# Weight conversion on GpSimd in halves, a new order in the weighted sum, and a new plan of when attention, conversion and reloads are emitted

## The chip, the cores and the metric

The kernel runs on one core of a Trainium2 chip. The metric is the time of one execution in device microseconds. It was run three times; a profiled execution of its own gives the trace.

## The reference, cut to what matters

```python
# q, k, v: (2, 8, 576, 64) float32
scores = scale * np.matmul(q, k.transpose(0, 1, 3, 2))
kth = np.partition(scores, -32, axis=-1)[..., -32:-31]
scores = np.where(scores >= kth, scores, -1e9)
attn = softmax(scores)                       # exp(scores - max) / (sum + 1e-9)
x = np.matmul(attn, v)                       # -> (1152, 512): tokens x (heads * 64)
h = x @ w_in                                 # (512, 2048)
g = h * np.tanh(softplus(h))
x = g @ w_out                                # (2048, 512)
out = ((x @ w_a) * (x @ w_b)) @ w_out2       # 512 -> 1536 -> 512
```

The five weight matrices arrive as float64. The kernel gets their bits and makes float32 numbers of them on the chip.

## The kernel before, in words

**Attention.** The 1152 tokens make nine tiles of 128 rows: tiles 0 to 3 are batch 0, tiles 5 to 8 batch 1, and tile 4 holds the last 64 rows of both. A tile has four pairs of heads, so there are 36 pairs, numbered here 0 to 35; pairs 16 to 19 are tile 4. Per pair, TensorE makes the scores (`psc`, L175), ScalarE copies them to SBUF, and VectorE finds the 32 largest of each row by four rounds of `max` (L191) and three of `match_replace` (L194), then masks the exponentials (`e`, L212). TensorE transposes the masked rows in nine chunks of 128 columns (`pe`, L220), three to a PSUM bank; ScalarE copies each bank (`et`, L221), and TensorE multiplies with `v` into `px` (L227). Chunks 0 to 3 belong to the pair's first head, 5 to 8 to its second, chunk 4 to both. After a tile's last pair, `prs` (L241) spreads the row sums, and the tile's `x` is ready.

**The MLPs.** `PLAN` cuts the tiles into three blocks. Block 0 is the tiles [0, 1] and then [2], block 1 the tiles [3, 4, 5], block 2 the tiles [6, 7, 8]. For each block `gated` runs 16 chunks of the first MLP (once for [0, 1] and once for [2] in block 0; products `ph` L355, sums `acc` L362), and `bilinear` runs 12 chunks of the second (`ph`, sums `po`). The two gated groups of block 0 work in plain float32, the rest in split fp32r: each weight unit is made into a high and a low part by a copy (L327, or L325 on VectorE) and a subtraction on GpSimd (L328).

**The weights.** They come as 68 units of 128x512. `convert_` loads a unit's 64-bit words (L281, `w64`, three buffers), ScalarE scales the high words (L286) and the low words (L287) and takes the sign (L290), VectorE shifts (L288), GpSimd adds (L291) and multiplies with the sign (L292), and the unit is stored to DRAM (L299). `weight_` reloads it from there (`raw`, L318, `BUFS[2]` buffers), or, for the first units, takes it from the buffer `w` where it was made (`BUFS[1]` buffers). All DMAs are issued by SP's one queue, in order. A `w64` buffer is free for the load three units on only when L292 has read it.

**What sets the order.** `together` interleaves two streams by their counts: the quarter steps of attention (four to a pair, 144 in all) and the chunks of an MLP group. `STEPS` says how many attention steps are spread over each group. `chunk` emits conversions ahead of need, `CONV[2]` sixteenths of a unit more per chunk. The framework then orders each engine's instructions by priorities and a timeline of its own; the result is a fixed list for each engine, executed in order.

Of the kernel before, what the change touches and what calls it, by code (L numbers as in the profile page):

```python
# [14 lines left out]
ALU = mybir.AluOpType  # L15
# [4 lines left out]
U = 512  # L20
# [16 lines left out]
ABUF = (5, 3, 2, 1, 2, 3, 1, 2)  # L37
COPIES = (0, 0, 0, 1, 4, 2)

CONV = (26, 28, 15, 2)  # L40

STEPS = (28, 25, 20, 26, 13, 0, 5)

BUFS = (3, 11, 5, 6, 1)

WIDE = {2 * P: 2, P: 4}
NEG = -3.0e38


@with_exitstack  # L50
def topk_attention_mlps(ctx: ExitStack, tc: tile.TileContext, q, k, v, w, out):
# [6 lines left out]
    nc = tc.nc  # L58
# [5 lines left out]
    J = 4  # L64
# [22 lines left out]
    def bank(name, n=512):  # L87
        return ps.tile([P, n], F32, name=name, tag="bank", padded_shape=[P, 512])
# [4 lines left out]
    def load_v(b):  # L93
        vt[b] = const.tile([P, H, J, D], F32, name=f"v{b}")
        v4[b] = const.tile([P, NP, 2, D], F32, name=f"v4{b}")
        nc.gpsimd.memset(v4[b], 0.0)
        for h in range(H):
            nc.sync.dma_start(vt[b][:, h], v[b, h, 0:SM, :].rearrange("(p j) d -> p j d", j=J))
        for s in range(2):
            nc.sync.dma_start(  # L100
                v4[b][s * R:(s + 1) * R, :, s, :],
                v[b, :, SM:S, :].rearrange("(a s) p d -> s p a d", s=2)[s],
            )

    def prep_k(b, hp):
        ks = wp.tile([P, 2, J, D], F32, name="ks", bufs=BUFS[4])
        kr = wp.tile([R, 2, D], F32, name="kr", bufs=BUFS[4])
        for s in range(2):
            nc.sync.dma_start(ks[:, s], k[b, 2 * hp + s, 0:SM, :].rearrange("(p j) d -> p j d", j=J))
        nc.sync.dma_start(kr, k[b, 2 * hp:2 * hp + 2, SM:S, :].rearrange("h p d -> p h d"))  # L110
        km = wp.tile([P, 2, J, 2, D], F32R, name="km", bufs=BUFS[4])
        kn = wp.tile([R, 2, 2, D], F32R, name="kn", bufs=BUFS[4])
        for z, raw in ((km, ks), (kn, kr)):
# [66 lines left out]
    def largest(s2):  # L180
# [6 lines left out]
        for r in range(TOPK // 8):  # L187
# [4 lines left out]
            if r < TOPK // 8 - 1:  # L192
                for s in range(2):
                    nc.vector.match_replace(wk[:, s, :], m8[:, s, got], src[:, s, :], NEG)  # L194
            if r == 0:
# [9 lines left out]
    def weighted_sum_(t, hp, s2, wk, e2, kth):  # L205
        if hp == 0:
            if t in (0, J):
                load_v(t // J)
            XR[t] = att.tile([P, NP, P], F32, name="xr", bufs=2), att.tile([P, H], F32, name="sm")
        xr, sm = XR[t]  # L210
        for s in range(2):
            nc.vector.scalar_tensor_tensor(e2[:, s, :], s2[:, s, :], kth[:, s:s + 1], e2[:, s, :],  # L212
                                           op0=ALU.is_ge, op1=ALU.mult, accum_out=sm[:, 2 * hp + s:2 * hp + s + 1])
        et = att.tile([P, 2 * J + 1, P], F32, name="et", bufs=ABUF[3])
        ef = e2.rearrange("p s c -> p (s c)")
        for g in range(3):
            pe = bank("pe", 3 * P).rearrange("p (i t) -> p i t", t=P)
            for i in range(3):
                n = 3 * g + i
                nc.tensor.transpose(pe[:, i, :], ef[:, n * P:(n + 1) * P], ident)  # L220
            nc.scalar.copy(et[:, 3 * g:3 * g + 3, :], pe)  # L221
        px = bank("px", P)
        for b, o, n in ([(t // (J + 1), 0, P)] if t != J else [(b, b * R, R) for b in range(B)]):
            for j in range(J + 1):
                for s in range(2):
                    i = s * (J + 1) + j
                    nc.tensor.matmul(px[s * D:(s + 1) * D, o:o + n],  # L227
                                     vt[b][:, 2 * hp + s, j, :] if j < J else v4[b][:, hp, s, :],
                                     et[:, i if j < J else J, o:o + n],
                                     start=(j == 0), stop=(j == J), skip_group_check=True)  # L230
        nc.scalar.copy(xr[:, hp, :], px)
        if hp == NP - 1:
            with tc.high_priority(PRI[5]):
                rs = att.tile([P, H], F32, name="rs")
                x = xp.tile([P, NP, P], F32, name="x", bufs=4)
                nc.vector.tensor_scalar(rs, sm, 1e-9, None, op0=ALU.add)
                nc.vector.reciprocal(rs, rs)
                pr = bank("prs")
                for h in range(H):
                    o = h % 2 * D  # L240
                    nc.tensor.matmul(pr[o:o + D, h // 2 * P:(h // 2 + 1) * P], rs[:, h:h + 1].to_broadcast([P, D]),  # L241
                                     ident, start=True, stop=True, skip_group_check=True)
                nc.vector.tensor_mul(x, xr, pr.rearrange("p (c t) -> p c t", t=P))
                X[t] = x
# [27 lines left out]
    def convert(n):  # L272
        with tc.high_priority(PRI[4]):
            convert_(n)

    def convert_(n):

        while len(stored) < min(n, len(order)):
            key = order[len(stored)]
            w64 = wp.tile([P, U], mybir.dt.int64, name="w64", bufs=BUFS[0])  # L280
            nc.sync.dma_start(w64, w[:, len(stored), :])  # L281
            high, low, highf, count = (w64.bitcast(dt).rearrange("p (n t) -> p n t", t=2)[:, :, i]
                                       for dt, i in ((I32, 1), (U32, 0), (F32, 1), (I32, 0)))
            wf = wp.tile([P, U], F32, name="w", bufs=BUFS[1])
            wi = wf.bitcast(I32)
            nc.scalar.mul(wf, highf, 2.0 ** -112)  # L286
            nc.scalar.activation(count, low, AF.Copy, scale=2.0 ** -29)  # L287
            nc.vector.tensor_scalar(wi, wi, 3, 0x7FFFFFFF, op0=ALU.logical_shift_left, op1=ALU.bitwise_and)  # L288
            if len(stored) % 4 < SIGN[key[0]]:
                nc.scalar.activation(highf, highf, AF.Sign)  # L290
                nc.gpsimd.tensor_tensor(wi, wi, count, op=ALU.add)  # L291
                nc.gpsimd.tensor_mul(wf, wf, highf)  # L292
            else:
                nc.vector.scalar_tensor_tensor(wi, high, -0x80000000, wi, op0=ALU.bitwise_and, op1=ALU.bitwise_or)
                nc.gpsimd.tensor_tensor(wi, wi, count, op=ALU.add)
            if len(stored) < made[3] + BUFS[1] - 2:
                fresh[key] = wf
            stored[key] = dp.tile([P, U], F32, name=f"ws{len(stored)}")
            nc.sync.dma_start(stored[key], wf)  # L299

    def chunk():

        convert(CONV[1] + made[2] * CONV[2] // 16)
        made[2] += 1
# [68 lines left out]
    def gated(block, tiles, yt, at, split, second):  # L373
# [9 lines left out]
        acc = [ps_a.tile([P, DM], F32, name="acc", tag="acc") for _ in tiles]  # L383
        K = WIDE.get(T, 1)
        for f0 in range(0, F1, K):
# [80 lines left out]
    att_stream = attention()  # L466
    steps = iter(STEPS)
    together(attend(4 * NP * len(PLAN[0][0][0][0])), (converting(CONV[0]), CONV[0]))
    for i, (groups, s2, s3) in enumerate(PLAN):
# [41 lines left out]
```

## Time and profile before

| | |
|---|---|
| median of 3 runs (lowest, highest) | 801.2 us (799.43, 801.82) |
| the profiled execution | 802.57 us |
| its span | 800.8 us |
| TensorE (PE) busy | 689.9 us (86%) |
| VectorE (DVE) busy | 613.8 us (77%) |
| GpSimd (POOL) busy | 475.1 us (59%) |
| ScalarE (ACT) busy | 520.0 us (65%) |
| mean granted TensorE clock | 0.93 |

The busy shares are averages over a span whose first and last halves have different limits; the forty slices and the windows by stage are to be read before any average.

### The profile page before, as it was taken

The page shows a single profiled execution, that of the slowest core. Times are in us where ns is not written, and L with a number is a line of the kernel's source. Part 1 is how long each engine was busy: PE and PEld are TensorE (multiplying, and loading weights), DVE is VectorE, ACT ScalarE, POOL GpSimd, SP SyncE. Part 2 cuts the span into 40 slices and gives each one's busy share as a digit, 9 for nine tenths or more (in the row PEclk, how much of TensorE's full clock was granted, in tenths as well). Part 3 has the DMA queues.
Part 4 walks back from the last instruction along what each step waited for, and adds up shares of the span by engine and source line. Part 5 has one row for each costly group of instructions (what it writes and reads, how often), then busy time and mean ns, then how long its engine had stood idle before and what let it go on. Part 6 is the DMA issues. An engine that isn't in the chain of part 4 may idle for free.

```text
span 800.8 us, 12319 instructions
## 1 busy us (share of the span) xinstructions
PE 689.9 (86%) x3988; PEld 575.0 (72%) x3988; DVE 613.8 (77%) x1224; ACT 520.0 (65%) x1118; POOL 475.1 (59%) x390
## 2 busy tenths in 40 slices
PE   3565656698888799889999999997999999989997
PEld 2443535565656577679998888886889999969996
DVE  2999999989999999999788899999811265523332
ACT  5887778788899865655656688886533265553232
POOL 5676656677775740146656556773556767665661
PEclk9996666789999799989999999999999999989999
DMA  7987566689899754353324234331233454433431
GB/s 222 280 268 226 179 202 188 192 227 332 237 324 320 236 188 121 103 143 91 103 70 132 80 106 119 96 103 41 90 95 95 129 171 118 133 105 94 134 102 39
DMA packets 78816, 124.80 MB, mean 156 GB/s; under 512 B 27424, under 2 KB 31520, under 8 KB 78752
## 3 DMA queue, kind: packets, MB, share of 16 engines
q1 hardware_dynamic: 78752, 124.02, 51.5%
q8 instruction: 31, 0.51, 0.3%
q14 instruction: 33, 0.27, 0.1%
HBM read 103.81 MB, written 20.19 MB: 155 GB/s over the span
## 4 chain that ended last, share of the span: by engine, by line
PE 57%; DVE 21%; DMA 9%; ACT 6%; issue 3%; POOL 2%; SPq 1%; ACTq 0%; POOLq 0%; DVEq 0%
PE ph L355 29%; PE po L362 9%; PE acc L362 9%; DVE m L191 8%; DVE wk L194 6%; DMA w<-in_w_dram 6%; PE px L227 4%; DMA raw<-ws 3%; DVE e L212 3%; PE psc L175 2%; DVE w L288 2%; PE pe L220 2%; POOL w L292 1%; ACT w L286 1%; PE prs L241 1%
## 5 line engine op out<-in xcount | busy, mean ns | idle before, releaser
L328 POOL TENSOR_TENSOR whl<-raw,whl 128x512 fp32r<-128x512 f32 x161 | 214.7, 1342 | 162.3 <-ACT whl L327 123.6
L191 DVE MAX8 m<-wk 128x8 f32<-128x576 f32 x216 | 157.8, 748 | 0.9
L355 PE MATMUL ph<-yh,whl 128*128 128x384 f32 x576 | 157.4, 345 | 1.2 <-ACT yh L337 0.7
L291 POOL TENSOR_TENSOR w<-w,w 128x512 int32<-128x512 int32 x68 | 90.9, 1337 | 77.4 <-DVE w L288 49.7
L355 PEld LDWEIGHTS ph<-yh,whl 128*128 128x128 f32 x576 | 107.0, 193 | 4.9 <-ACT yh L337 1.0
L194 DVE MATCH_REPLACE8 wk<-m,wk 128x576 f32<-128x576 f32 x144 | 106.3, 740 | 0.0
L355 PE MATMUL ph<-yl,whl 128*128 128x384 f32 x288 | 98.7, 343 | 0.0
L292 POOL TENSOR_TENSOR w<-w,w 128x512 f32<-128x512 f32 x68 | 93.2, 1373 | 5.4 <-ACT w L290 1.2
L327 ACT CAST whl<-raw 128x512 fp32r<-128x512 f32 x110 | 67.9, 622 | 40.0 <-PE ph L355 17.2
L227 PE MATMUL px<-et,v 128*64 128x128 f32 (+1 forms) x800 | 78.9, 309 | 15.7 <-ACT et L221 15.6
L227 PEld LDWEIGHTS px<-et,v 128*64 128x64 f32 x800 | 57.0, 159 | 36.9 <-ACT et L221 21.9
L212 DVE SCALAR_TENSOR_TENSOR e<-s,m,e 128x576 f32<-128x576 f32 x72 | 77.6, 1085 | 0.9 <-ACT e L198 0.5
L370 POOL TENSOR_TENSOR gl<-m,gh 128x384 fp32r<-128x384 f32 x52 | 55.9, 1074 | 36.5 <-PE po L362 12.1
L220 PE MATMUL pe<-ident,e 128*128 128x128 f32 x324 | 56.3, 312 | 23.1 <-DVE e L212 15.6
L427 DVE TENSOR_TENSOR m<-ph,e 128x384 f32<-128x384 f32 x36 | 20.0, 556 | 70.7 <-PE ph L355 70.3
L369 ACT CAST gh<-m 128x384 fp32r<-128x384 f32 x68 | 34.8, 512 | 56.7 <-DVE m L427 36.2
L355 PE MATMUL ph<-xh,whl 128*128 128x384 f32 x256 | 71.3, 339 | 0.0
L175 PE MATMUL psc<-kks,qh 128*128 128x288 f32 x160 | 55.1, 364 | 17.7 <-ACT kks L126 8.9
L286 ACT ACTIVATE w<-w 128x512 f32<-128x512 f32 x68 | 46.1, 677 | 34.2 <-DMA w<-in_w_dram 22.5
L191 DVE MAX8 m<-s 128x8 f32<-128x576 f32 x72 | 53.5, 750 | 18.8 <-ACT s L177 18.6
L220 PEld LDWEIGHTS pe<-ident,e 128*128 128x128 f32 x324 | 44.7, 161 | 30.9 <-issue 8.5
L177 ACT COPY s<-psc 128x288 f32<-128x288 f32 x144 | 51.6, 402 | 16.0 <-PE psc L175 15.7
(87 smaller groups left out, 1484.7 us busy)
## 6 DMA issues: line engine op xcount, KB each, us to landing
raw<-ws SPq DMA_DIRECT2D x224, 256.0 KB, 2.7
w<-in_w_dram SPq DMA_DIRECT2D x68, 512.0 KB, 4.3
ws<-w SPq DMA_DIRECT2D x68, 256.0 KB, 4.5
qr<-in_q_dram SPq DMA_DIRECT2D x16, 256.0 KB, 4.0
ks<-in_k_dram SPq DMA_DIRECT2D x16, 128.0 KB, 3.8
v<-in_v_dram SPq DMA_DIRECT2D x16, 128.0 KB, 4.2
out_dram<-o SPq DMA_DIRECT2D x8, 256.0 KB, 2.6
qr<-in_q_dram SPq DMA_DIRECT2D x4, 128.0 KB, 5.5
```

The lines of the kernel that those rows point to most:

```text
L175: nc.tensor.matmul(psc, qq[:, s, :], kk[:, a * HS:(a + 1) * HS], start=(n == 0), stop=(n == len(parts) - 1))
L191: nc.vector.max(m8[:, s, got], src[:, s, :])
L194: nc.vector.match_replace(wk[:, s, :], m8[:, s, got], src[:, s, :], NEG)
L212: nc.vector.scalar_tensor_tensor(e2[:, s, :], s2[:, s, :], kth[:, s:s + 1], e2[:, s, :], op0=ALU.is_ge, op1=ALU.mult, accum_out=sm[:, 2 * ...
L220: nc.tensor.transpose(pe[:, i, :], ef[:, n * P:(n + 1) * P], ident)
L227: nc.tensor.matmul(px[s * D:(s + 1) * D, o:o + n], vt[b][:, 2 * hp + s, j, :] if j < J else v4[b][:, hp, s, :], et[:, i if j < J else J, o ...
L291: nc.gpsimd.tensor_tensor(wi, wi, count, op=ALU.add)
L292: nc.gpsimd.tensor_mul(wf, wf, highf)
L327: nc.scalar.copy(wh, raw)
L328: sub().tensor_sub(wl, raw, wh.bitcast(F32))
L355: nc.tensor.matmul(ph, a, x, start=(i == 0), stop=(i == len(mm) - 1))
L362: nc.tensor.matmul(acc[i], z[:, i * P:(i + 1) * P], a, start=(first and m == 0), stop=(last and m == len(mm) - 1))
```

## The change

GpSimd's add and multiply of a unit are each issued as two instructions on 256 columns (`PIECES`). The weighted sum takes the column chunks of `et` from the last to the first and the second head before the first, with the shared chunk last; the sum is the same, in another order of addition. `CONV[2]` goes from 15 to 20, `BUFS[1]` (buffers `w`) from 11 to 9, `BUFS[2]` (buffers `raw`) from 5 to 9, and `STEPS` spreads fewer attention steps over the two gated groups of block 0 and more over its bilinear group.

```diff
-CONV = (26, 28, 15, 2)
+CONV = (26, 28, 20, 2)
-STEPS = (28, 25, 20, 26, 13, 0, 5)
+STEPS = (24, 14, 32, 28, 14, 0, 5)
-BUFS = (3, 11, 5, 6, 1)
+BUFS = (3, 9, 9, 6, 1)
+PIECES = 2
...
         for b, o, n in ([(t // (J + 1), 0, P)] if t != J else [(b, b * R, R) for b in range(B)]):
-            for j in range(J + 1):
-                for s in range(2):
+            for nth, j in enumerate((*range(J - 1, -1, -1), J)):
+                for s in (1, 0):
...
-                                     start=(j == 0), stop=(j == J), skip_group_check=True)
+                                     start=(nth == 0), stop=(nth == J), skip_group_check=True)
...
+        pieces = [slice(i * U // PIECES, (i + 1) * U // PIECES) for i in range(PIECES)]
...
-                nc.gpsimd.tensor_tensor(wi, wi, count, op=ALU.add)
-                nc.gpsimd.tensor_mul(wf, wf, highf)
+                for z in pieces:
+                    nc.gpsimd.tensor_tensor(wi[:, z], wi[:, z], count[:, z], op=ALU.add)
+                for z in pieces:
+                    nc.gpsimd.tensor_mul(wf[:, z], wf[:, z], highf[:, z])
```

**TensorE, around `prs` of tile 4.** Line numbers in the change are a few higher (L227 is L230 there, L241 is L244, L355 is L362, L362 is L369). Before, the place reads:

```order
L227 MATMUL px<-et,v_331 64x64 x3
L241 MATMUL prs<-ident,rs 64x128 x8
L227 MATMUL px<-et,v_331 64x64 x5
L227 MATMUL px<-et,v_332 64x64 x2
L227 MATMUL px<-et,v_2611 64x64 x8
L227 MATMUL px<-et,v_2612 64x64 x2
L143 MATMUL pq<-ident,qr 128x128 x2
L362 MATMUL acc<-raw,m_3085 128x512 x4
```

In the change the same `prs` stands among the products of the bilinear group (`yl_1206` is the low part of its input):

```order
L362 MATMUL ph<-yl_1206,whl 128x384
L230 MATMUL px<-et,v_339 64x64
L244 MATMUL prs<-ident,rs 64x128 x8
L230 MATMUL px<-et,v_339 64x64 x7
L230 MATMUL px<-et,v_340 64x64 x2
L230 MATMUL px<-et,v_3024 64x64 x8
L230 MATMUL px<-et,v_3025 64x64 x2
L145 MATMUL pq<-ident,qr 128x128 x2
L369 MATMUL po<-whl,gl_3589 128x512 x3
```

Before, the sums of the gated group [2] (`acc`) still stand behind tile 4's last `px`; in the change both gated groups are done there, and products (`ph` from `yl`) and sums (`po`) of the bilinear group stand on the two sides of it.

**SP's queue, where the reloads of the first gated group begin** (the numbers at `w` and `ws` name buffers and DRAM tiles). Before:

```order
L299 DMA ws_1809<-w 128x512
L318 DMA raw<-ws_794 128x512
L281 DMA w_2026<-in_w_dram 128x512
L299 DMA ws_1828<-w 128x512
L281 DMA w_2045<-in_w_dram 128x512
L299 DMA ws_1937<-w 128x512
L318 DMA raw<-ws_809 128x512
L281 DMA w_2223<-in_w_dram 128x512
```

And in the change, where they begin two conversions earlier:

```order
L306 DMA ws_1639<-w 128x512
L325 DMA raw<-ws_856 128x512
L325 DMA raw<-ws_912 128x512
L285 DMA w_1764<-in_w_dram 128x512
L306 DMA ws_1660<-w 128x512
L285 DMA w_1832<-in_w_dram 128x512
L306 DMA ws_1741<-w 128x512
L325 DMA raw<-ws_957 128x512
L325 DMA raw<-ws_972 128x512
L285 DMA w_1853<-in_w_dram 128x512
```

Where one reload stood between two conversions, there are now often two. From the load of unit 38 to that of unit 68 the queue holds 30 reloads before and 52 in the change; in the whole program 224 and 229.

## Rows read from the trace of the kernel before

**Rows 1.** The page: busy time of each engine, and two lines of its 40 slices.

```profile
PE 689.9 (86%) x3988; PEld 575.0 (72%) x3988; DVE 613.8 (77%) x1224; ACT 520.0 (65%) x1118; POOL 475.1 (59%) x390
...
DVE  2999999989999999999788899999811265523332
...
PEclk9996666789999799989999999999999999989999
```

**Rows 2.** Windows by stage: busy us of each engine, clock, DMA share, GB/s.

```profile
core 0: us, PE busy (x) PEld busy (x) DVE busy (x) ACT busy (x) POOL busy (x), PEclk, DMA share, GB/s
140.00:300.00 160.00, 132.18 (x694) 94.77 (x695) 153.57 (x304) 134.64 (x282) 108.91 (x95) 0.89 0.83 257
350.00:601.00 251.00, 245.42 (x1542) 215.35 (x1540) 211.79 (x418) 166.35 (x370) 148.49 (x119) 0.99 0.33 93
601.00:800.80 199.80, 191.41 (x971) 174.47 (x970) 77.05 (x133) 81.62 (x160) 121.12 (x95) 0.98 0.38 112
```

**Rows 3.** Waits of PE and of DVE, 136 to 350 us (total, times, longest).

```profile
PE px L227 <- ACT et L221: 12.2, 6, 4.1
PE ph L355 <- DMA raw<-ws: 8.0, 7, 2.4
...
DVE w L288 <- POOL w L292: 2.7, 1, 2.7
```

**Rows 4.** Timeline of PE where the last `px` of pairs 16 and 20 run.

```profile
304.22 1.26 PE L227 MATMUL px<-et,v 128*64 128x64 f32 x34
...
347.48 1.68 PE L227 MATMUL px<-et,v 128*64 128x128 f32 x14
```

**Rows 5.** The window from pair 16's last `px` to pair 35's.

```profile
305.30:601.20 295.90, 283.15 (x1859) 244.32 (x1854) 255.06 (x514) 194.55 (x438) 157.34 (x126) 0.98 0.35 98
```

**Rows 6.** PE's price: chain, timeline, and two tiles (ns min/median/max).

```profile
648.76 2.10 PE ph L355 x12
650.86 2.08 PE acc L362 x9
...
301.25 1.06 PE L355 MATMUL ph<-xf,raw 128*128 128x128 f32 x8
170.73 5.31 PE L362 MATMUL acc<-w,m 128*128 128x512 f32 x12
...
L355 PE MATMUL ph<-xf,raw x216: 271/275/483, 167.5 to 325.4; 128*128 128x128 f32 x64, 128*128 128x256 f32 x44
L362 PE MATMUL acc<-raw,m x80: 590/592/894, 179.9 to 341.1; 128*128 128x512 f32 x80
```

**Rows 7.** DVE's first instruction of a gated set of 512 columns (busy, mean ns).

```profile
L397 DVE TENSOR_SCALAR e<-ph 128x512 f32<-128x512 f32 x12 | 8.1, 678 | 0.0
```

**Rows 8.** POOL's instructions by form (first two), then two of its timeline.

```profile
L291 POOL TENSOR_TENSOR w<-w,w 128x512 int32<-128x512 int32 x68 | 90.9, 1337 | 77.4 <-DVE w L288 49.7 <-ACT w L287 8.6 <-ACT w L290 4.7
L116 POOL TENSOR_TENSOR kn<-kr,kn 64x128 fp32r<-64x128 f32 x4 | 2.5, 630 | 0.0
...
8.79 1.28 POOL L291 TENSOR_TENSOR w<-w,w 128x512 int32<-128x512 int32 x1 [0.42 <-ACT kn L115]
10.03 0.45 POOL L116 TENSOR_TENSOR kn<-kr,kn 64x128 fp32r<-64x128 f32 x1
```

**Rows 9.** SP's queue: its longest wait, 140 to 300 us, and loads of units 38 and 68.

```profile
SPq L281 <- POOL w L292: 57.6, 29, 4.2
...
161.18 0.57 SPq L281 DMA_DIRECT2D w<-in_w_dram  x1
...
276.24 0.43 SPq L281 DMA_DIRECT2D w<-in_w_dram  x1
```

**Rows 10.** Windows of the conversion stretch, with DMA share and GB/s last.

```profile
161.00:276.20 115.20, 99.23 (x504) 68.27 (x504) 108.81 (x217) 102.04 (x212) 81.79 (x69) 0.92 0.89 278
...
200.00:250.00 50.00, 42.68 (x227) 29.31 (x228) 48.56 (x97) 44.60 (x93) 35.14 (x28) 0.97 0.92 279
220.00:230.00 10.00, 8.62 (x44) 5.14 (x40) 10.00 (x21) 9.31 (x18) 6.79 (x6) 1.00 1.01 372
```

More of the change, by code (lines that the diff above doesn't have):

```diff
@@ L290, in convert_ @@
                 nc.scalar.activation(highf, highf, AF.Sign)
-                nc.gpsimd.tensor_tensor(wi, wi, count, op=ALU.add)
-                nc.gpsimd.tensor_mul(wf, wf, highf)
+                for z in pieces:
+                    nc.gpsimd.tensor_tensor(wi[:, z], wi[:, z], count[:, z], op=ALU.add)
+                for z in pieces:
+                    nc.gpsimd.tensor_mul(wf[:, z], wf[:, z], highf[:, z])
             else:
                 nc.vector.scalar_tensor_tensor(wi, high, -0x80000000, wi, op0=ALU.bitwise_and, op1=ALU.bitwise_or)
-                nc.gpsimd.tensor_tensor(wi, wi, count, op=ALU.add)
+                for z in pieces:
+                    nc.gpsimd.tensor_tensor(wi[:, z], wi[:, z], count[:, z], op=ALU.add)
             if len(stored) < made[3] + BUFS[1] - 2:
```

## The prediction

> **What bounds the kernel now.** I read the page first [rows 1]. Its busy shares name no limit: TensorE has 86%, VectorE 77%. The slices do. VectorE stands at 9 almost without a break from slice 3 to about slice 18, a slice being 20 us, while TensorE's granted clock is often below 1, which is what an engine with gaps shows. From slice 18 on the clock is full and VectorE falls to 5 and below. So the kernel has two halves: first the top-k search on VectorE sets the pace, then TensorE's products do.
>
> The windows by stage make that a measure [rows 2]. From 140 to 300 us VectorE is busy 153.6 of 160 us and the clock is 0.89. From 350 to 601 us TensorE is busy 245.4 of 251 us at clock 0.99, and from 601 to the end nearly as much, with VectorE at 77 of 200. The waits agree [rows 3]: between 136 and 350 us TensorE waits 12.2 us for the copies of `et` and 8.0 us for reloads, and VectorE's longest wait is 2.7 us in all.
>
> A time is thus gained where TensorE's MLP work is moved from the second half into the gaps of the first, and lost where VectorE, before the handover, gets more to do or to wait for. I take the last `px` of pair 16 as the mark of the handover: it ends at 304.22 + 1.26 = 305.5 us; that of pair 20 ends at 349.2 [rows 4], and that of pair 35, the last, at 601.2, where the window of [rows 5] is cut. Behind pair 16 come 800.8 - 305.5 = 495.3 us.
>
> **The change part by part.**
>
> *Attention and MLP in another order (STEPS, CONV).* Both lists hold the same matmuls, but for a few that read `raw` in place of `w`; what differs is how many MLP products stand ahead of a given pair. I price them by TensorE's spacing [rows 6]: 2.10 / 12 = 0.174 us for a split product of 384 columns, 2.08 / 9 = 0.231 us for one of 512; a plain float32 product leaves two records, and from start to start I get (1.06 - 0.275) / 7 = 0.112 us at 128 columns and (5.31 - 0.59) / 11 = 0.429 us at 512 (the run without its last record, through the number of steps). A chunk of the gated group [2] has 8 of the first and 2 of the second, 1.75 us; a chunk of the bilinear group 24 x 0.174 + 9 x 0.231 = 6.26 us. Counted in the order, 73.6 us of MLP work stand ahead of pair 16's last `px` before and 84.9 us in the change: 11.3 us more, six and a half chunks of group [2], so both gated groups are done. At pair 20 it is 85.8 against 129.6 us, seven bilinear chunks more; at pair 35 the lists agree again within 0.2 us.
>
> So 11.3 us leave the stretch behind pair 16. Besides, between pairs 16 and 20 TensorE took 349.2 - 305.5 = 43.7 us for 12.2 us of MLP work and 25.5 us of attention, 6.0 us of it gaps. In the change 70 us of work stand there, so the gaps can be filled. Between 6.0 and nothing I take half, 3.0, since the copies that `px` waits for remain. Gain: 14.3 us if pair 16 comes no later.
>
> VectorE allows it: from 305.3 to 601.2 us it is busy 255.1 of 295.9 us [rows 5], so a stretch shorter by 14.3 still leaves it 26 us.
>
> *What makes pair 16 later.* The MLP's own VectorE work moves with it: ahead of pair 16's masks stand 2.5 more gated sets, each of two instructions of 0.68 us [rows 7] (the second taken as the first), 3.4 us, and one more search instruction, about 1 us. VectorE is the bound there, so all 4.4 us count.
>
> *GpSimd in halves.* No row has 256 columns, so I bound it [rows 8]. Undisturbed, 512 columns took 1.28 us and 128 columns 0.45, which is 2.16 ns a column and 0.73 us for 256: four make 2.92 where two made 2.56, +0.36 us a unit. By the means, 0.630 and 1.337, a half costs 0.87 and a unit 3.46 in place of 2.67, +0.79 us. GpSimd itself has room: 108.9 of 160 us [rows 2], and 40 units would add 14 to 32. But the conversion is a loop: SP's load of a unit waits for the multiply of the unit three before, 57.6 us in 140 to 300 us [rows 9]. Through three buffers a unit gets 0.12 to 0.26 us longer, over 30 units 3.6 to 7.9 us, if nothing in the loop has slack. Behind the waiting load stand the stores and the reloads, in SP's one queue; and VectorE's shift (L288), in order, holds up the search if its unit is late.
>
> *Reloads.* Nine buffers let SP run further ahead, two `w` buffers fewer make five reloads more, 224 to 229. What counts is where they stand: from the load of unit 38 to that of unit 68, 115 us before [rows 9], the queue has 22 more reloads of 0.262 MB, 5.8 MB. The stretch moved 278 GB/s x 115.2 us = 32.0 MB at share 0.89 [rows 10]; now it is 37.8 MB. At the rate of 200 to 250 us (279 GB/s at 0.92, so 303 at full share) this takes 125 us, 9.6 more; at the 372 GB/s of the best ten microseconds it takes 102, and nothing is added. The Trainium skill ("DMA: Bandwidth & Descriptors", Specifications) gives about 358 GB/s as the HBM limit of a core; by it the stretch would take 106 us, and the sum would have no term for the feed; the ten microseconds at 372 lie slightly above that figure, the mean of the stretch far below.
>
> Halves and reloads lengthen the same loop, so they cost the larger of the two and not both: 0 to 9.6 us. I take 2, near the low end, because the row nearest to it, VectorE's waits for the conversion at today's load, is 2.7 us in all.
>
> *The weighted sum backwards.* All ten products now wait for the last copy of `et`; before, the first three could go earlier, and the scheduler put the next `q` transposes behind them. Of TensorE's 12.2 us of waiting for `et` before the handover [rows 3] none sets the pace, and after it other products stand between. I count 0; the bounds are a gain of 3 us, the gaps that I left above, and a loss of as much.
>
> **The sum.** 800.8 - 11.3 - 3.0 + 4.4 + 2.0 = 792.9 us of span. The profiled execution took 802.57, 1.8 more than its span, and the median of the runs is 1.4 less than that; so 793 us as a median. About 0.3%, 2.4 us, is what a measurement of this kernel can tell from no change.
>
> **The rivals.**
>
> *The feed takes the gain back.* DMA is at 0.89 and VectorE at 94% of the conversion stretch [rows 10]; ask 18% more bytes of it and the reloads come late, TensorE's queue stands at a product, and scores and pair 16 with it. With the full 9.6 us instead of 2.0 the sum is 800.5 us of span, and if the gaps stay too, 803. For it speaks that the fifty microseconds at 0.92 moved only 279 GB/s; against it, that TensorE waited but 8.0 us for reloads and will have nine of them ahead. Chance 0.17.
>
> *VectorE stalls at the shifts: slower.* The change's order bunches the conversions: between the masks of pairs 10 and 13 VectorE has 18 shifts, where the densest three pairs before have 16. At (276.24 - 161.18) / 30 = 3.84 us a unit [rows 9] and 0.26 for the halves, 18 units take 73.8 us, against 61.4 for 16 today: 12.4 us, and VectorE, in order, can't search meanwhile. With the 4.4 us pair 16 then comes 16.8 us later, and the kernel takes 800.8 - 14.3 + 16.8 = 803.3 us, 806 if the gaps stay. It decides from a delay of pair 16 of 17 us on. For it speaks the wait of 57.6 us in SP's queue; against it, that a bunch can be followed by pairs with fewer units, in which the loop catches up, but VectorE can't get back what it lost. Chance 0.23.
>
> *More than I count.* From 140 to 300 us the clock is 0.89 of full [rows 2], which is 160 x 0.11 = 17.6 us of TensorE's time. If the denser products win back half of it, pair 16 comes 8.8 us earlier, and with all 6.0 us of gaps filled the sum is 781 us. For it speaks that more products stand in the same gaps; against it, that VectorE, which sets the pace there, gains nothing by the clock. Chance 0.15, within the faster ones.
>
> *The moves do nothing,* since the lists agree again at pair 35: it would need TensorE to have no gaps ahead of pair 20, against the gaps that [rows 4] show; I put it with the first rival.
>
> **How the numbers follow.** My case, 788 to 798, has 0.45 and the larger gain 0.15, so 0.60 for faster; the feed rival, centred on no change, is the 0.17 within 0.3%, and the stall is the 0.23 for slower. The range goes from 781 (the larger gain) to 805 (the stall, short of its worst end); the likeliest case alone has 788 to 798.
>
> **What would show it.** In the changed profile the last `px` of pair 16 should end at about 312 us, and from there to the end take about 481 us, with VectorE's window behind it busier than 86%. A half on GpSimd should take 0.73 to 0.87 us. The last load of a unit, at 276.2 us now [rows 9], should go out at 277 to 287. If pair 16 comes after 318 us, and VectorE's waits at L288 before 300 us exceed 10 us, the stall is right; if TensorE's waits for reloads grow beyond 15 us with a DMA share near 1, the feed is. If the tail behind pair 35, 199.6 us, has changed by more than 2 us, something moved that I have not seen.

## The result, and the profile after

| | before | changed |
|---|---|---|
| median of 4 runs (lowest, highest) | 800.32 us (799.31, 801.82) | 805.99 us (805.4, 807.11) |
| span of the profiled execution | 800.8 us | 803.7 us |

The ratio is 1.0078, with a 95% interval from 1.0055 to 1.01: slower, by more than the 0.3% that can be told from no change. The forecast said faster, 793 us. The two profiled executions lie 2.9 us apart, less than the medians; the accounts below are of these two.

The windows of the changed kernel, cut at the same stages as [rows 2] and at its own mark, the last `px` of pair 16 (columns as there):

```profile
core 0: us, PE busy (x) PEld busy (x) DVE busy (x) ACT busy (x) POOL busy (x), PEclk, DMA share, GB/s
140.00:300.00 160.00, 130.95 (x709) 95.37 (x706) 145.10 (x287) 136.92 (x282) 127.05 (x171) 0.92 0.88 289
604.10:803.70 199.60, 191.08 (x969) 174.18 (x968) 76.43 (x133) 82.40 (x160) 121.70 (x95) 0.98 0.36 106
314.00:604.10 290.10, 268.60 (x1807) 238.16 (x1802) 250.76 (x518) 185.64 (x426) 148.29 (x120) 0.96 0.31 86
314.00:410.00 96.00, 93.37 (x666) 86.39 (x661) 80.04 (x167) 54.95 (x127) 51.67 (x42) 0.98 0.35 92
410.00:570.00 160.00, 141.13 (x916) 122.58 (x915) 154.19 (x320) 115.83 (x268) 75.28 (x62) 0.94 0.30 86
```

The mark itself, on PE's timeline of the changed kernel (start, duration, both in us), answers to [rows 4]:

```profile
312.80 1.39 PE L230 MATMUL px<-et,v 128*64 128x64 f32 x40 [0.73 <-ACT et L223]
```

Pair 16 ends at 312.80 + 1.39 = 314.2 us, 8.7 later than before; 803.7 - 314.2 = 489.5 us follow in place of 495.3, 5.8 fewer. The forecast had 6.4 later and 14.3 fewer. The tail behind pair 35 is unchanged, 199.6 us.

The stretch from pair 16 to pair 35 tells where the gain went, set beside [rows 5]. TensorE's busy time fell from 283.15 to 268.60 us, 14.6, more than the 11.3 that I priced. Of that, 12.8 us are block 0's gated products (7.3 `acc`, 5.5 `ph`), which no longer stand behind the mark: the work did move ahead. Yet up to the mark TensorE's busy time rose by 4.1 us only (215.73 to 219.84, in the windows further down), for its `px` there cover 29.8 us in place of 41.5; the weighted sum, in the part on the prediction, comes back to this. But TensorE's idle time rose from 12.75 to 21.5 us, where I had let it fall by 3.0. And it is not idle where it used to be: before 410 us, in the stretch with the gaps that I wanted filled, 2.6 us are left; from 410 to 570 us it is idle for 18.9. In those two stretches VectorE does the opposite: it stands still for 16.0 of the first 96 us, and in the second it works 154.2 of 160. The kernel before, in the same 96 and 160 us behind its own pair 16, has TensorE idle for 7.9 and 4.9 us, and VectorE for 7.0 and 12.8:

```profile
305.30:401.30 96.00, 88.13 (x616) 75.21 (x612) 89.03 (x192) 56.84 (x133) 38.13 (x30) 0.95 0.39 108
401.30:561.30 160.00, 155.13 (x988) 134.92 (x987) 147.24 (x286) 120.45 (x268) 95.89 (x77) 1.00 0.33 94
```

The waits of PE in that stretch name the place (total us, times, longest), first of the changed kernel, 314 to 604 us:

```profile
PE psc L177 <- ACT qh L155: 6.3, 6, 2.4
PE psc L177 <- DVE ql L156: 6.1, 5, 3.1
PE px L230 <- ACT et L223: 4.1, 4, 1.7
PE ph L362 <- DVE yl L346: 1.8, 1, 1.8
```

and of the kernel before, 305 to 601 us:

```profile
PE px L227 <- ACT et L221: 4.8, 3, 2.1
...
PE psc L175 <- DVE x L243: 1.4, 1, 1.4
PE psc L175 <- ACT xr L231: 0.8, 1, 0.8
PE psc L175 <- ACT qh L153: 0.7, 1, 0.7
PE psc L175 <- DVE ql L154: 0.7, 2, 0.4
```

The scores (`psc`) wait for the two parts of the transposed queries (`qh`, `ql`): 1.4 us before, 12.4 now, 11.0 more. With what else the scores waited for before, 2.2 us in these lines and 0.3 for keys, the rise is 8.5, nearly all of the 8.75 us by which the idle time rose. One such wait on the changed kernel's two timelines, PE first, then DVE:

```profile
541.90 0.44 PE L145 MATMUL pq<-ident,qr 128*128 128x128 f32 x2
542.92 0.53 PE L177 MATMUL psc<-kks,qh 128*128 128x288 f32 x2 [0.58 <-ACT qh L155]
546.59 0.85 PE L177 MATMUL psc<-kks,ql 128*128 128x288 f32 x2 [3.14 <-DVE ql L156]
```

```profile
543.55 1.40 DVE L193 MAX8 m<-wk 128x8 f32<-128x576 f32 x2
544.88 0.66 DVE L246 TENSOR_TENSOR x<-xr,prs 128x512 f32<-128x512 f32 x1
545.47 0.75 DVE L193 MAX8 m<-wk 128x8 f32<-128x576 f32 x1
546.14 0.40 DVE L156 SCALAR_TENSOR_TENSOR ql<-pq,qh 128x256 fp32r<-128x256 f32 x1
```

The queries are transposed by 541.90 + 0.44 = 542.3 us. VectorE makes `ql` at 546.1, because the search, and once a tile's `x`, stand ahead of it in its queue; TensorE has no product in between and waits 3.14 us. The opposite happens earlier, on DVE's timeline of the same kernel:

```profile
407.93 0.76 DVE L193 MAX8 m<-s 128x8 f32<-128x576 f32 x1 [4.93 <-ACT s L179]
```

Here the search waits 4.93 us for scores, which stand in TensorE's queue among bilinear products. In all VectorE waits 11.5 us for scores between 300 and 420 us.

Ahead of pair 16, VectorE's windows up to the mark, before and changed:

```profile
0.00:305.50 305.50, 215.73 (x1168) 156.56 (x1169) 281.87 (x579) 243.81 (x520) 196.59 (x169) 0.85 0.78 240
```

```profile
0.00:314.00 314.00, 219.84 (x1221) 163.00 (x1221) 281.15 (x575) 251.94 (x533) 229.41 (x311) 0.88 0.79 255
```

VectorE has no more work there, 281.15 against 281.87 us; it stands still 9.2 us longer. Its waits from 137 us to pair 16, before and changed:

```profile
DVE w L288 <- POOL w L292: 2.7, 1, 2.7
DVE w L288 <- ACT w L286: 1.2, 1, 1.2
DVE w L288 <- POOL w L291: 1.1, 1, 1.1
DVE m L191 <- ACT s L177: 0.6, 2, 0.4
DVE w L288 <- issue: 0.5, 1, 0.5
```

```profile
DVE w L292 <- ACT w L290: 4.7, 6, 1.5
DVE m L409 <- ACT m L408: 3.2, 2, 1.8
DVE w L292 <- POOL w L298: 2.6, 2, 1.3
DVE w L292 <- issue: 1.0, 2, 0.7
```

The shifts of the conversion (L292, before L288) wait 8.3 us where they waited 5.5, and the gated sets 3.2 where they did not wait. From the start of the program the shifts wait 16.3 us, 13.7 before. GpSimd's halves, to be read beside [rows 8], took 800 ns:

```profile
L298 POOL TENSOR_TENSOR w<-w,w 128x256 f32<-128x256 f32 x136 | 106.1, 800 | 1.5 <-ACT xr L234 1.1 <-ACT w L294 0.4
```

### The profile page after: what moved, and what is told of

It is laid out like the page before. It is cut to its first block, busy times and chain, and to the rows that moved or that the text cites. A ratio compares the mean times of both kernels' runs of the same rounds, so it can differ in the third digit from the quotient of the medians.

```text
span 803.7 us, 12499 instructions
## 1 busy us (share of the span) xinstructions
PE 679.5 (85%) x3988; PEld 575.3 (72%) x3988; DVE 608.3 (76%) x1224; ACT 520.0 (65%) x1118; POOL 499.4 (62%) x526
## 5 line engine op out<-in xcount | busy, mean ns | idle before, releaser
L335 POOL TENSOR_TENSOR whl<-raw,whl 128x512 fp32r<-128x512 f32 x164 | 217.5, 1334 | 138.4 <-ACT whl L334 102.7
L362 PE MATMUL ph<-yh,whl 128*128 128x384 f32 x576 | 157.9, 344 | 0.7 <-ACT yh L344 0.7
L296 POOL TENSOR_TENSOR w<-w,w 128x256 int32<-128x256 int32 x136 | 106.0, 800 | 68.2 <-DVE w L292 37.8
L362 PEld LDWEIGHTS ph<-yh,whl 128*128 128x128 f32 x576 | 107.5, 193 | 3.9 <-ACT yh L344 1.5
L298 POOL TENSOR_TENSOR w<-w,w 128x256 f32<-128x256 f32 x136 | 106.1, 800 | 1.5 <-ACT xr L234 1.1
L362 PE MATMUL ph<-yl,whl 128*128 128x384 f32 x288 | 99.1, 344 | 1.8 <-DVE yl L346 1.8
L377 POOL TENSOR_TENSOR gl<-m,gh 128x384 fp32r<-128x384 f32 x52 | 57.5, 1106 | 41.5 <-ACT gh L376 13.9
L230 PE MATMUL px<-et,v 128*64 128x128 f32 (+1 forms) x800 | 59.4, 293 | 24.7 <-ACT et L223 24.7
L230 PEld LDWEIGHTS px<-et,v 128*64 128x64 f32 x800 | 47.9, 152 | 37.5 <-ACT et L223 30.3
L214 DVE SCALAR_TENSOR_TENSOR e<-s,m,e 128x576 f32<-128x576 f32 x72 | 72.8, 1014 | 1.4 <-ACT e L200 1.0
L362 PE MATMUL ph<-xh,whl 128*128 128x384 f32 x256 | 71.2, 340 | 1.2 <-DVE m L409 1.0
L177 PE MATMUL psc<-kks,ql 128*128 128x288 f32 x160 | 51.5, 362 | 17.7 <-DVE ql L156 17.6
L177 PEld LDWEIGHTS psc<-kks,qh 128*128 128x128 f32 x160 | 34.8, 228 | 41.9 <-ACT qh L155 30.7
```

The lines of the kernel that those rows point to most:

```text
L177: nc.tensor.matmul(psc, qq[:, s, :], kk[:, a * HS:(a + 1) * HS], start=(n == 0), stop=(n == len(parts) - 1))
L230: nc.tensor.matmul(px[s * D:(s + 1) * D, o:o + n], vt[b][:, 2 * hp + s, j, :] if j < J else v4[b][:, hp, s, :], et[:, i if j < J else J, o ...
L296: nc.gpsimd.tensor_tensor(wi[:, z], wi[:, z], count[:, z], op=ALU.add)
L298: nc.gpsimd.tensor_mul(wf[:, z], wf[:, z], highf[:, z])
L335: sub().tensor_sub(wl, raw, wh.bitcast(F32))
L362: nc.tensor.matmul(ph, a, x, start=(i == 0), stop=(i == len(mm) - 1))
```

## The experiments

In each, "before" is the kernel before on the same chip, in the same session; ratios are to it, with their 95% interval. Pair 11, 16 and 35 with a time mean the start of the last record of their `px` in the profiled execution, which is 0.2 to 0.3 us before its end; so counted, the kernel before has 305.3 and 601.2 for the last two, the changed one 314.0 and 604.1.

**One part undone in the source.** The first four put back `STEPS` (e1), whole units (e2) or `BUFS` (e3) in the changed kernel, or gave the kernel before the new `STEPS` (e4).

```diff
-STEPS = (24, 14, 32, 28, 14, 0, 5)
+STEPS = (28, 25, 20, 26, 13, 0, 5)
...
-PIECES = 2
+PIECES = 1
...
-BUFS = (3, 9, 9, 6, 1)
+BUFS = (3, 11, 5, 6, 1)
```

> The changed kernel with the old STEPS alone put back; in the order, 85 us of MLP work stand ahead of pair 20's last px, as before the change, where the changed kernel has 130. Theory of the order (the new STEPS put bilinear chunks of block 0 ahead of the attention of tiles 4 and 5, so VectorE starves at 360 to 420 us and TensorE later runs out of products at 420 to 450 and 520 to 560): the loss goes, 794 to 801 us, and TensorE is busy over 95% from pair 22 to pair 31. Theory of the feed (halves and reloads make pair 16 8.5 us later and this carries through to the end): 804 to 808 us, pair 16 at 312 us or later.

> The changed kernel with whole units on GpSimd (PIECES = 1). Theory of the order: 803 to 808 us, no measurable gain, with the same gaps at 420 to 450 and 520 to 560 us. Theory of the feed: pair 16 at 306 to 309 us and 798 to 802 us in all.

> The changed kernel with the old BUFS (5 reload buffers, 11 w buffers). Theory of the order: 803 to 808 us. Theory of the feed: fewer reloads ahead of the last conversions, pair 16 at 306 to 310 us, 798 to 802 us in all.

> The kernel before with the new STEPS alone. Theory of the order: it has the whole loss, 804 to 809 us, with TensorE short of products near pairs 23 to 25 and 30 to 31. Theory of the feed: 799 to 802 us, no change.

Measured: 816.19 us (1.0176 [1.0143, 1.0209]), 821.42 (1.025 [1.0225, 1.0275]), 830.49 (1.0362 [1.0336, 1.0387]) and 817.14 (1.0188 [1.0163, 1.0213]), before 801.12. All four miss what every theory expected: each mixture is slower than both kernels. One edit makes the framework order every engine anew, so these runs price a new order and not the part. From here on the order of every engine was written down and forced, and only the edits that are named were made in it.

**The changed order forced, and one edit undone in it.** e5 forces the changed kernel's own order; e6 has whole units in it, e8 the old order of the sum.

```diff
+    dep = mybir.DependencyInfo(mybir.DependencyClass.NoSync, mybir.DependencyReason.DATA)
...
+                if last is not None:
+                    tc.add_manual_dep(made[engine][at], last.name, dep, reason="pinned")
+                last = made[engine][at]
```

> The changed kernel with the order of every engine's instructions written down and forced, nothing else changed. It is the base for the runs that change one thing while no instruction moves. Both theories: 803 to 809 us, as the changed kernel (806.0), px of pair 16 at 312 to 316, of pair 35 at 602 to 606. Outside of that the forcing itself costs or gives something, and the pinned runs have to be read against this one alone.

> The changed kernel's order forced, but GpSimd converts each unit whole (one instruction of 512 columns in place of two of 256; the other engines' orders stay word for word). GpSimd is then 0.42 us a unit shorter for 68 units, 28 us in all. Theory A (the capped lead: behind pair 22 VectorE paces the attention and TensorE starves, the halves are a small price at the front): pair 16 at most 3 us earlier, the end 0 to 3 us earlier than the pinned base, 803 to 806. Rival B (the feed: the halves and the reloads delay the front and that is where the gain went): pair 16 6 to 10 us earlier and the end by as much, 796 to 800.

> The changed kernel's order forced; the weighted sum takes the transposed columns first to last again, as the kernel before did. Theory A: nothing that can be measured, within 2 us of the pinned base. Rival C (the backwards sum makes each px wait for the last eviction at its first matmul, where the forward order had eight matmuls to hide it): 3 to 8 us earlier than the pinned base, most of it between pairs 9 and 16 where px waits for et.

Measured, with before at 801.96: e5 805.07 (1.0043 [1.0025, 1.0062]), pair 16 at 315.1, pair 35 at 605.9: a fair base. e6 808.94 (1.0092 [1.0061, 1.0122]), pair 16 at 316.6; e8 805.78 (1.0053 [1.003, 1.0077]), pair 16 at 314.5. Both rivals fall: neither the halves nor the backwards sum make this order slower. Theory A missed e6 as well, by a little: whole units were to be as fast or faster. The same edit as in e2 costs 3.9 us where nothing moves, against some 14 there, by the ratios.

**Less search on VectorE.** e7 for pairs 23 to 31, e16 for every pair from 17 on, both in the changed order; e18 is the control in the order of before.

```diff
+            n = S // 2 if r and 17 <= i else S
...
-                nc.vector.max(m8[:, s, got], src[:, s, :])
+                nc.vector.max(m8[:, s, got], src[:, s, :n])
...
-                    nc.vector.match_replace(wk[:, s, :], m8[:, s, got], src[:, s, :], NEG)
+                    nc.vector.match_replace(wk[:, s, :n], m8[:, s, got], src[:, s, :n], NEG)
```

> The changed kernel's order forced; for pairs 23 to 31 the search's rounds after the first look at the first 288 of 576 columns only (so these pairs' sums differ from the reference), which takes some 3.7 us of VectorE's work from each of the 9 pairs and leaves all else alone. Nothing ahead of pair 23 changes. Theory A: TensorE stood idle for some 19 us between 418 and 564 us since VectorE could not bring products in time; it gets 10 to 19 us of it back: 787 to 796, and TensorE's busy share of 418 to 564 goes above 95%. Rival B: what is lost was lost ahead of pair 16, the end moves by less than 4 us, 802 or more.

> The changed kernel's forced order with the search's later rounds over the first 288 columns for every pair from 17 on (these pairs' sums differ from the reference), 70 us of VectorE's work in all. If VectorE's own work sets the pace behind pair 22: pair 16 to pair 35 falls from 290.8 to 270 to 277 us, the end to 786 to 793. If the order does (TensorE reaches instructions of the attention whose inputs come a fixed chain later, and has no product to put in between): TensorE still idles 10 us or more between 410 and 570 and the end is 796 to 800, hardly below the 800.3 of the run that cut pairs 23 to 31.

> The control for the short search: the kernel before with its own order forced and the search's later rounds over 288 columns for every pair from 17 on (these pairs' sums differ from the reference). In the changed order this gave 12.1 us. If the moves are what made VectorE the pace behind pair 16: here 0 to 6 us, 795 to 801, most of it ahead of pair 20 where VectorE was full. If VectorE paces either order alike: 10 to 14 us, 787 to 791.

Measured: e7 800.28 (0.9992 [0.9969, 1.0015]), 4.8 us below the base, between the two theories; the pairs around those nine kept their full search. e16 792.94 (0.991 [0.9885, 0.9936]), before 800.85. e18 797.45 (0.9959 [0.9934, 0.9983]), before 801.67, within what was expected if the moves made VectorE the pace. e16 lands between its two theories: its time is within the first one's bounds, at their upper end, and its stretch of 278.3 us just beyond them, but TensorE still idles 14.0 us between 410 and 570, as the second one said. The windows from pair 16 to pair 35 in e5, e16 and e18:

```profile
315.10:605.90 290.80, 267.64 (x1808) 237.47 (x1802) 250.84 (x518) 185.12 (x426) 149.05 (x120) 0.96 0.29 86
```

```profile
317.70:596.00 278.30, 263.28 (x1807) 234.63 (x1802) 204.94 (x516) 184.88 (x426) 148.10 (x120) 0.98 0.30 90
```

```profile
303.60:594.50 290.90, 279.75 (x1861) 242.69 (x1855) 203.35 (x507) 194.52 (x438) 157.52 (x126) 0.99 0.35 100
```

VectorE lost about the same work in both, 46 and 52 us of the stretch. In the changed order that makes the stretch 12.5 us shorter, in the old one 5.0 (from the 295.9 of [rows 5]). By the ratios the whole kernel gains 1.3% against its base in the one, 0.4% in the other; there the base is the kernel before as it was, since its order was not forced without an edit. So VectorE does set the pace behind pair 16 in the changed order, for the larger part, and only a little in the old one. The scores' wait for `qh` and `ql` in that stretch falls from 11.6 to 4.7 us, and TensorE's idle time from 23.2 to 15.0; the rest of it does not come from VectorE's amount of work.

**The products spread later.** e9 and e10 keep e5's instructions, but the MLP's stand later among the attention's, by this rule for the time t at which each ran:

```
e9:   t 335 -> 335, 410 -> 432, 460 -> 460, linear between
e10:  t 335 -> 335, 410 -> 432, 460 -> 460, 525 -> 545, 550 -> 550
```

> The changed kernel's forced order with one thing altered: the MLP's instructions that ran between 335 and 460 us (on all engines and in SP's queue) stand later among the attention's, up to 22 us at 410, so that 10 to 15 us less of the MLP's products lie ahead of pairs 20 to 22 and as much more ahead of pairs 23 to 25. Theory A, restated after the short search gave 4.8 us only: TensorE and VectorE take turns as the bound. From 340 to 410 TensorE is full and VectorE waits for scores, from 410 to 450 the products have run out and TensorE waits for the attention. Then TensorE's idle time between 410 and 460 falls from 7.8 us to 3 or less and the end comes 4 to 7 us earlier than the pinned base: 798 to 801. Rival B (the loss is that of the front alone, the order behind it costs nothing): within 2 us of the base, 803 to 807.

> As the run before, and the same for the second place: the MLP's instructions between 460 and 550 us stand up to 20 us later among the attention's, so that 7 to 11 us less of the products lie ahead of pairs 27 to 30 and the two pairs without any product (30 and 31) get some. Theory A: the idle 12 us between 510 and 570, and part of the low granted clock there, go as well: 786 to 794, below both kernels. If VectorE's own work is the bound from 440 to 570 (it is 18 to 20 of 20 us busy there), only the first place pays: 797 to 801. Rival B: 803 to 807.

Measured, before 802.61: 821.63 (1.0229 [1.0196, 1.0261]) and 825.9 (1.0291 [1.0261, 1.0321]); both theories miss. In e10 TensorE's idle time from 510 to 570 us did go, from 12.6 to 3.0 at full clock, but the gain was eaten elsewhere. The windows of e9 and e10 from pair 16 to pair 35 say where:

```profile
312.90:622.50 309.60, 287.40 (x1807) 242.74 (x1804) 254.25 (x518) 187.03 (x426) 151.18 (x120) 0.95 0.28 82
```

```profile
313.70:626.80 313.10, 292.45 (x1809) 237.82 (x1804) 254.45 (x518) 186.72 (x426) 149.94 (x120) 0.97 0.28 81
```

Beside e5 there are as many matmuls and 20 to 25 us more of TensorE's busy time. The rule put the products singly between the attention's matmuls; the groups of PE, for e9 from 335 to 470 us and for e5 from 335 to 455, show what that does to `px`:

```profile
L230 PE MATMUL px<-et,v 128*64 128x128 f32 (+1 forms) x199 | 20.5, 269 | 1.1 <-ACT et L223 1.1
```

```profile
L230 PE MATMUL px<-et,v 128*64 128x128 f32 (+1 forms) x192 | 10.9, 255 | 1.7 <-ACT et L223 1.7
```

The records of some 195 cover 20.5 us in place of 10.9. A group's busy time also counts what runs beside it, so the price is better read from starts on the timeline of e9:

```profile
463.19 0.43 PE L230 MATMUL px<-et,v 128*64 128x128 f32 x2
463.55 0.49 PE L369 MATMUL acc<-whl,gl 128*128 128x512 f32 x1
463.98 0.43 PE L230 MATMUL px<-et,v 128*64 128x128 f32 x2
```

From one `px` product (two records) to the next pass 0.79 us. The product of 512 columns between them takes 0.231 in a run [rows 6], so the single `px` adds 0.56 us; in a run, ten of them (x20) took 1.31 in the changed kernel. These two runs thus do not test the lead of the products; that a smoother order would be faster stays open.

**The front: reload bytes and load buffers.** e11 halves the bytes of block 0's gated reloads, e14 gives the unit loads five buffers.

```diff
-            nc.sync.dma_start(raw, stored[key])
+            rows = P if split else P // 2
+            raw = raw[:rows]
+            nc.sync.dma_start(raw, stored[key][:rows])
...
-            nc.tensor.matmul(ph, a, x, start=(i == 0), stop=(i == len(mm) - 1))
+            nc.tensor.matmul(ph, a, x[:a.shape[0]], start=(i == 0), stop=(i == len(mm) - 1))
...
-BUFS = (3, 9, 9, 6, 1)
+BUFS = (5, 9, 9, 6, 1)
```

> The changed kernel's forced order; the reloads of block 0's gated part bring 64 of the 128 rows of a unit and its products sum over 64 rows (half of that sum is left out), so each of these reloads moves 128 KB in place of 256. Theory F (the feed: 72 reloads lie ahead of 310 us where 49 did, the DMA engines are 90 to 99% busy from 180 to 300 us, and VectorE's wait for unit conversions there is the front's delay): pair 16 comes 5 to 10 us earlier than the base's 315.1, and the end 5 to 10 us earlier, 795 to 800. Rival: the front is late because VectorE and ScalarE have more to do ahead of pair 16: pair 16 within 2 us of the base, the end within 2 us.

> The changed kernel's forced order with five buffers for the unit loads in place of three; no instruction moves. Ahead of pair 16 VectorE's shifts wait for ScalarE, which waits for the unit loads, and the loads wait in SP's queue for GpSimd to release a load buffer (46.7 us of such waits between 137 and 314 us). Theory L (these three buffers hold the front back): pair 16 comes 4 to 8 us earlier than the base's 315.1 and the end by as much, 797 to 801. Theory D (the DMA engines, 99% busy from 180 to 210 us, hold it back): the loads only queue there, pair 16 within 2 us of the base, 803 to 807.

Measured: e11 has a ratio of 1.0247 [1.0199, 1.0295], from two of its six executions (820.9 and 823.7 us; the others took 846 to 865), and a span of 822.0: slower than any theory allowed. Up to pair 11 it can be read: that ends at 229.1, the base's at 231.5, so half the bytes gave 2.4 us, in one profile of each. Then its granted clock fell, as its windows show:

```profile
180.00:210.00 30.00, 29.66 (x120) 18.05 (x120) 23.80 (x47) 27.14 (x53) 25.53 (x35) 1.00 0.95 293
240.00:270.00 30.00, 28.33 (x104) 18.78 (x103) 21.79 (x44) 19.19 (x40) 15.47 (x25) 0.56 0.72 221
```

In the base the second window has clock 0.85. e14 took 804.73 us (1.0052 [1.0028, 1.0077]), the base's time; in its profile pair 16 is at 311.3, 3.8 us earlier, which the medians do not confirm. Neither the reloads' bytes nor the load buffers are shown to explain the late front.

**The edits in the order of before.** e12 has nine reload buffers, e17 the halves, e13 both and the backwards sum, e15 five load buffers besides. No instruction moves.

```diff
-BUFS = (3, 11, 5, 6, 1)
+BUFS = (3, 11, 9, 6, 1)
```

> The kernel before with its own order forced, and nine reload buffers in place of five; no instruction moves. Theory F says that the buffers alone do little while the reloads stand where they stood: within 3 us of the kernel before, 798 to 804. Rival: early reloads crowd out the unit loads by themselves: pair 16 more than 4 us late and 805 or more. Second rival: the wait of products for reloads was a cost of the kernel before: 796 or less.

> The kernel before with its own order forced, and the change's three edits that need no move: halves on GpSimd, the last transposed columns first, nine reload buffers. What is left out of the change is the moved instructions (and nine in place of eleven unit buffers). If the loss lies in the moves (theory M): 794 to 800, as fast as or faster than the nine buffers alone (799.0 beside 802.6), so that the moves cost the changed kernel 6 to 10 us. If the halves or the backwards sum cost what the forecast feared: 801 or more.

> The run with the three edits in the order of before, and five load buffers as well. Theory L: 2 to 4 us faster than with three load buffers, 791 to 797, below both kernels. Theory D: within 1.5 us of the run with three.

> The kernel before with its own order forced and GpSimd's halves alone. The three edits in this order cost 18.6 us beside the nine buffers alone; their pair 16 was 9.4 us late, which five load buffers took back, and behind pair 16 they lost 9 us in which px waits for the last eviction. If the first part is the halves (a unit holds its load buffer 0.84 us longer on GpSimd) and the second the backwards sum: pair 16 at 310 to 316, pair 16 to the end as in the kernel before (495 us), 805 to 812 in all. If the halves cost nothing in this order either, as in the changed one: pair 16 at 304 to 307, 799 to 803, and the whole 18.6 us lie with the backwards sum.

Measured: e12 798.97 (0.9959 [0.9938, 0.9981]), before 802.61; e13 817.57 (1.0206 [1.018, 1.0232]) and e15 810.91 (1.0124 [1.0097, 1.0152]), before 800.85; e17 800.44 (0.998 [0.9956, 1.0004]), before 801.67. e12, with the nine buffers, is faster than the kernel before by 0.4%. How much of that is the buffers' is open: the order of before was not forced without an edit, e17 in the same forced order is at 0.998, and TensorE's waits for reloads from 136 to 350 us did not fall in e12 (9.8 us, before 8.0). The halves cost nothing that can be measured. The theory that all the loss lies in the moves falls with e13: by difference from e12 the halves and the backwards sum cost some 2.5%, 20 us, in the old order, and as the halves were free in e17, I put it down to the backwards sum. That sum was not run alone, and what it costs together with the halves was not separated. PE's wait for the copies of `et`, 140 to 604 us, in e13:

```profile
PE px L229 <- ACT et L223: 34.9, 22, 7.4
```

In the kernel before the same window has 12.2 us in 6 waits. e15's five load buffers make it 6.7 us faster than e13, more than either theory had, and bring pair 16 back to 304.8 from 315.3; yet its pair 35 is at 611.7 us, 10.5 after the kernel before.

## Why the prediction was wrong, point by point

**The step that failed is "VectorE allows it".** I took VectorE's 26 us of slack behind pair 16 as an average over the stretch, and let TensorE fill its gaps with nothing lost later. The work moved, TensorE's busy time fell by 14.6 us, and the gaps ahead of pair 20 were filled, both as forecast. But TensorE, full with the bilinear products between 314 and 410 us, handed VectorE its scores late, and VectorE's slack was spent there, 16.0 us of standing still. From 410 to 570 us VectorE was 96% busy and TensorE waited for it. In place of 3.0 us less idle time there were 8.75 more, 11.75 on the wrong side, of which the larger fall in busy time (14.6 for 11.3) gave back 3.3; so the gain of 14.3 came out as 5.8. e16 and e18 show that VectorE's work limits this stretch now, for the larger part, and hardly did before; that the early products are what turned it round is read from the two timelines, and no run with another lead alone confirms it.

**Pair 16** came 8.7 us later, forecast 6.4. The size is near, the reasons are not: the 4.4 us of more VectorE work do not show (281.15 against 281.87 us), and all of the delay is VectorE waiting, 9.2 us more. What has a name in it is 3.2 us at the gated sets, where I had priced their work and not their wait, 2.8 at the shifts from 137 us on, and small waits for the rest. My term of 2.0 for the conversion rested on "2.7 us in all" of waits at the shifts; that was the longest single wait, and together they were 5.5. What delays the shifts was not settled: e11 and e14 moved pairs 11 and 16 by 2 to 4 us, and neither changed the end for the better.

**The halves** took 800 ns, within 0.73 to 0.87, and cost nothing at the end in either order (e17; e6, without them, is if anything slower). GpSimd had the room.

**The backwards sum** I counted at 0 with bounds of 3 us. In the changed order that holds (e8). In the old order it does not, by far (e13): what covers it, as I read it, is the place of `px` among other matmuls, and the new order gives it that. I also missed a gain: with as many records, TensorE was busy 679.5 us in place of the 689.9 of [rows 1], and its `px` cover less, before and changed:

```profile
PE 679.5 (85%) x3988; PEld 575.3 (72%) x3988; DVE 608.3 (76%) x1224; ACT 520.0 (65%) x1118; POOL 499.4 (62%) x526
```

```profile
L227 PE MATMUL px<-et,v 128*64 128x128 f32 (+1 forms) x800 | 78.9, 309 | 15.7 <-ACT et L221 15.6
L230 PE MATMUL px<-et,v 128*64 128x128 f32 (+1 forms) x800 | 59.4, 293 | 24.7 <-ACT et L223 24.7
```

A pair's `px` now stand in one run more often (pair 20 has x20, where [rows 4] shows its last x14), and e9 showed what single ones cost. Most of this is the order's and not the sum's: with the old sum in it, TensorE was busy 683.9 us (e8). Behind pair 16 it did not become time, since TensorE's idle time rose.

**The reloads.** "Nine buffers" I had only as a load on the DMA engines; in the old order the run with them was 0.4% faster, part of which may be the forcing. The signs of the feed rival are absent: PE's waits for reloads from 136 to 350 us fell from 8.0 to 4.4. The DMA share of 140 to 300 us rose from 0.83 to 0.88. The page's slices of the changed kernel, 20 us each:

```profile
GB/s 233 283 268 234 210 195 188 114 299 334 355 271 315 312 291 119 41 104 145 70 104 101 82 91 94 118 54 0 159 27 92 131 170 110 139 107 93 131 53 39
```

From 180 to 220 us it moved 334 and 355 GB/s, where the 279 of [rows 10] had made me think of 303 as a ceiling. The Trainium skill's figure for a core's HBM limit ("DMA: Bandwidth & Descriptors", Specifications), about 358 GB/s, lay nearer; by it the feed's term was 0. These slices stay below that figure; the best ten microseconds before, 372 [rows 10], do not.

**The stall rival** was to be recognised by pair 16 after 318 us and by over 10 us of waits at the shifts before 300 us. Pair 16 was at 314.2. The second sign could tell nothing: those waits came to 16.3 us, but to 13.7 in the kernel before already, and from 137 us on to 8.3 against 5.5. Its direction was right, and its 806 near by luck: most of what the forecast missed, 8.5 of 10.8 us of span, was lost behind pair 16. That the moves do nothing is refuted by the filled gaps. Of the larger gain only the clock came, 0.92 in place of 0.89 from 140 to 300 us, and that not reliably: the profiled execution has a mean of 0.933 over the span, the three others 0.90 to 0.91, the kernel before 0.930. VectorE gained nothing by it. The other signs I named stand as said or at their edge: VectorE 86% busy behind pair 16, the tail unchanged, the last unit load at 287.3 us on the timeline of SP's queue:

```profile
287.27 0.33 SPq L285 DMA_DIRECT2D w<-in_w_dram  x1
```

What the moves alone cost: the changed order with the old sum is at 1.0053 (e8), the old order with the old sum and nine buffers at 0.9959 (e12). If the halves are free, the moved order, with two `w` buffers fewer, costs about 0.9%, 7.5 us. With the backwards sum it is the other way round (e13 1.0206, e5 1.0043). The edits' prices do not add up; they depend on the order.

## What to carry to other kernels

When work of one engine is moved ahead to fill its gaps, follow the engine that feeds it pair by pair, not by its average slack: ask which of its inputs now stand behind the moved work, and what that engine will owe later. Where an edit lets a framework order everything anew, force the order before pricing the edit, in the old order as well as in the new; a part undone in the source alone measures another kernel. Run the forced order of either kernel once without any edit, as the base for the rest; here the old one lacks it.

## What the runs showed of the hardware that I had not expected

- Products over 64 rows took as long as over 128 (median 376 against 379 ns, and 590 against 592). In the run with them, e11, the granted clock was 0.56 from 240 to 270 us, where TensorE was busy 28.3 of 30 us, against 0.85 in the base with 25.1. Ahead of it, from 180 to 210, it had been busy 29.7 of 30 at clock 1.00. A window's 0.56 is a mean of the two levels, 2.4 and 1.2 GHz. It was seen in one profile, and that the 64 rows are the cause was not tested.
- A `px` product set singly between two products of the MLP added 0.56 us to TensorE's time, against 0.13 in a run of ten (x20 in 1.31 us). The two orders with such places, e9 and e10, had 20 to 25 us more busy time for the same 1808 records.
- A half of 256 columns on GpSimd took 800 ns on average where 512 took 1337 [rows 8]: two halves cost 1.2 times the whole.
